# Strided sparse attention and a multiplicative FFN on one core: reordering the head's loads, casts and work

## The chip, the cores and the metric

The kernel runs on one core of one Trainium2 chip. The metric is the time of one execution on the device, in microseconds (us), as the median of several runs. The core has five engines that work side by side, each through its own queue in order: TensorE (PE, matrix multiplications and transposes into PSUM), VectorE (DVE), ScalarE (ACT), GpSimd (POOL) and SyncE (SP, which here only issues loads). 16 DMA engines move data between HBM and SBUF.

## The reference

Inputs are q, k, v of shape (8 batches, 8 heads, 576 positions, 64), and the weights w1, w2 (512 x 1024), w3 (1024 x 1024) and w_out (1024 x 512), all in float32. Heads 0 to 3 attend to the last 32 positions, heads 4 to 7 to every 32nd one back.

```
scores = q @ k.T / sqrt(64)
mask   = (0 <= i - j < 32)                   for heads 0..3
         (i >= j) and i % 32 == j % 32       for heads 4..7
attn   = softmax(where(mask, scores, -1e9)) @ v
x      = attn, heads side by side: (4608, 512)
out    = ((x @ w1) * (x @ w2)) @ w3 @ w_out  # (4608, 512)
```

## The kernel before

**The three kinds of work.** First, the *fold*: since h @ w3 @ w_out = h @ (w3 @ w_out), the kernel computes w34 = w3 @ w_out once. w3 comes in eight blocks of 128 rows (`load_w3(jc)`, called w3_0 to w3_7 in the text), w_out in four pieces (`load_wo(g)`). For a block, `fold_tr` (L357) transposes its eight 128 x 128 parts into one PSUM tile, which VectorE (L359) and ScalarE (L360) copy into w3T; `fold_mm` then multiplies w3T with w_out in two halves of four matmuls (L335, a "half step"), and the result is copied into w34 by VectorE or ScalarE. The list `fold` holds 23 units: for each block a half step, the transposes of the next block, and the other half step.

Second, *attention*, in 32 pairs of heads: pairs 0 and 1 of each batch are local, 2 and 3 strided. For a pair, `ph_T` (T) transposes q and k (L214) into one PSUM tile and copies them to qT and kT; `ph_R` (R, L230) does it for the last 64 positions of all heads of a batch; `ph_S` (S) makes the scores in two groups (L248), the exponential on ScalarE (L253) and the mask multiply on VectorE (L255); `ph_PV` (PV, L268) multiplies with v, whose extra column of ones gives the sum of the softmax, and VectorE divides (L274, L276); `ph_T2` (T2, L284) transposes the result, and a copy (L291 for strided pairs) puts it into xT. T, R and T2 share the PSUM pool psM, which has one buffer, so each waits until the one before has been copied out. S and PV share psB, which has two.

Third, the *FFN* in nine tiles of 512 tokens. `ab_halves` gives 16 units: x @ w1 (aps, L312, copied by ScalarE, L315) and x @ w2 (bps, L321, multiplied with the copy by VectorE, L323) for each of eight blocks of 128 columns. `o_halves` gives 8 units that multiply the product with w34 (L335) and store the result (L346, L347). Nine FFN tiles of 512 tokens cover eight batches of 576; the first tile needs batch 0's attention complete.

**The order of the work.** TensorE's instructions keep the order in which the program writes them. The attention phases of all batches stand in one list, `stream`; batch 0's are its first 21 units. `host(units, upto, lead)` writes out fold or FFN units one by one, and after each unit past the first `lead` ones puts in an even share of the stream units up to position `upto`. Before, batch 0's 21 units lie between fold units 4 to 23 (lead=3). In the first FFN tile, 8 units of batch 1 lie behind the ab units 10 to 16, and the remaining ones up to the end of batch 1's position (17 units) between the eight o units.

**Loads and casts.** All loads are issued by SP in the order of the calls, into the pool stgp of 9 buffers ("st"); a load waits until the cast of the load nine before has freed its buffer. A cast from float32 to float16 follows each: on GpSimd for w3, w_out, w2, q, k and the rest ("r", the last 64 positions of q and k), in `load_vL` and `load_vS` for v of the local and the strided heads; on ScalarE for w1. `copy(eng, ...)` picks the engine: "a" is L70, "v" L72 and "p" L74. The local heads' v needs a copy of its last 32 rows shifted to the first 32 partitions; that copy is on VectorE (L182). Since each engine works in order, a cast on GpSimd also waits for all casts of earlier loads.

Of the kernel before, what the change touches and what calls it, by code (L numbers as in the profile page):

```python
# [19 lines left out]
def kernel(  # L20
# [11 lines left out]
    nc = tc.nc  # L32
    B, H, S, D = q.shape
# [3 lines left out]
    P = 128  # L37
# [10 lines left out]
    LQ, LT = 96, 6  # L48
# [14 lines left out]
    AHEAD = 2  # L63

    def pe(ins):
        return tc.keep_in_program_order(ins)

    def copy(eng, out, in_):
        if eng == "a":
            nc.scalar.copy(out=out, in_=in_)  # L70
        elif eng == "v":
            nc.vector.tensor_copy(out=out, in_=in_)  # L72
        else:
            nc.gpsimd.tensor_copy(out=out, in_=in_)  # L74
# [47 lines left out]
    w1h = consts.tile([P, KM, DF], FP16)  # L122
    w2h = consts.tile([P, KM, DF], FP16)
# [9 lines left out]
    def load_wo(g, eng):  # L133
        src = moe_w_out.rearrange("(c p) n -> p c n", p=P)
        st = stgp.tile([P, 2, DM], FP32, tag="stg")
        nc.sync.dma_start(st, src[:, 2 * g:2 * g + 2, :])
        copy(eng, woh[:, 2 * g:2 * g + 2, :], st)

    def load_w3(jc, eng):
        st = stgp.tile([P, DF], FP32, tag="stg")  # L140
        nc.sync.dma_start(st, moe_w3[bass.ds(jc * P, P), :])
        t = ffn.tile([P, DF], FP16, tag="w3n", bufs=4)
        w3n[jc] = t
        copy(eng, t, st)

    def load_w12(g):
        cs = bass.ds(g * 256, 256)
        for wd, wh, eng in ((moe_w1, w1h, "a"), (moe_w2, w2h, "p")):
            st = stgp.tile([P, KM, 256], FP32, tag="stg")
            nc.sync.dma_start(st, wd.rearrange("(c p) n -> p c n", p=P)[:, :, cs])  # L150
            copy(eng, wh[:, :, cs], st)
# [4 lines left out]
    def load_qk(b, grp, engs="pp"):  # L156
        for nm, ten, eng in (("q", q, engs[0]), ("k", k, engs[1])):
            st = stgp.tile([P, 4, 4, D], FP32, tag="stg")
            nc.sync.dma_start(st.rearrange("p h c d -> p h (c d)"),
                              ten[b, 4 * grp:4 * grp + 4, 0:NM].rearrange("h (p c) d -> p h (c d)", c=4))  # L160
            t = qkp.tile([P, 4, 4, D], FP16, tag=f"{nm}{grp}")
            copy(eng, t, st.rearrange("p h c d -> p c h d"))
            x16[(b, nm, grp)] = t

    def load_rest(b, eng="p"):
        st = stgp.tile([P, H, D], FP32, tag="stg")
        for i, ten in enumerate((q, k)):
            nc.sync.dma_start(st[64 * i:64 * i + 64], ten[b, :, NM:S].rearrange("h p d -> p h d"))
        t = qkp.tile([P, H, D], FP16, tag="r")
        copy(eng, t, st)  # L170
        x16[(b, "r")] = t

    def load_vL(b):
        vt = v16L[b % 2]
        for hp in range(2):
            hs = slice(2 * hp, 2 * hp + 2)
            st = stgp.tile([P, 2, LT, D], FP32, tag="stg")
            for h in range(2):
                nc.sync.dma_start(st[32:P, h], v[b, 2 * hp + h].rearrange("(t p) d -> p t d", p=LQ))
            for pr in (bass.ds(32, 32), bass.ds(64, 64)):  # L180
                nc.gpsimd.tensor_copy(out=vt[pr, hs, :, 0:D], in_=st[pr])  # L181
            nc.vector.tensor_copy(out=vt[0:32, hs, 1:LT, 0:D], in_=vt[96:P, hs, 0:LT - 1, 0:D])  # L182

    def load_vS(b):
        vt = v16S[b % 2]
        for hp in range(2):
            st = stgp.tile([SQ, 2, ST, D], FP32, tag="stg")
            sf = st.rearrange("p h c d -> p h (c d)")
            sv = v[b, 4 + 2 * hp:6 + 2 * hp].rearrange("h (p c) d -> p h (c d)", c=ST)
            nc.sync.dma_start(sf[0:64], sv[0:64])  # L190
            nc.sync.dma_start(sf[64:SQ], sv[64:SQ])
            nc.gpsimd.tensor_copy(out=vt[:, 2 * hp:2 * hp + 2, :, 0:D], in_=st)  # L192
# [104 lines left out]
    def ab_halves(tch):  # L297
        tok = bass.ds(tch * NT, NT)
        res = []

        def first():
            abts[tch] = ffn.tile([P, KF, NT], FP16, tag="abt", bufs=4, name=f"abt{tch}")

        for jc in range(KF):
            st = {}

            def a(jc=jc, st=st):
                if jc == 0:
                    first()
                aps = psF.tile([P, NT], FP32, tag="f")  # L310
                for ci in range(KM):
                    pe(nc.tensor.matmul(aps, w1h[:, ci, bass.ds(jc * P, P)], xT[ci][:, tok],  # L312
                                        start=(ci == 0), stop=(ci == KM - 1)))
                asb = ffn.tile([P, NT], FP32, tag="asb")
                nc.scalar.copy(out=asb, in_=aps)  # L315
                st["asb"] = asb

            def bb(jc=jc, st=st):
                bps = psF.tile([P, NT], FP32, tag="f")
                for ci in range(KM):  # L320
                    pe(nc.tensor.matmul(bps, w2h[:, ci, bass.ds(jc * P, P)], xT[ci][:, tok],  # L321
                                        start=(ci == 0), stop=(ci == KM - 1)))
                nc.vector.tensor_mul(abts[tch][:, jc, :], bps, st["asb"])  # L323

            res += [a, bb]
        return res
# [45 lines left out]
    batch_end = {}  # L372
# [4 lines left out]
    for b in range(B):  # L377
# [4 lines left out]
        for i in range(4):  # L382
            p = 4 * b + i
# [14 lines left out]
    pos = [0]  # L398

    def host(units, upto, lead=0):  # L400
        n = len(units) - lead
        p0 = pos[0]
        for i, u in enumerate(units):
            u()
            tgt = p0 + ((upto - p0) * max(i + 1 - lead, 0)) // n
            while pos[0] < tgt:
                stream[pos[0]]()
                pos[0] += 1
# [2 lines left out]
    load_w3(0, "p")  # L411
    for g in range(4):
        load_wo(g, "p")
    load_w3(1, "p")
    load_qk(0, 0)
    load_rest(0)
    load_w3(2, "p")
    load_vL(0)
    load_w3(3, "p")
    load_qk(0, 1)  # L420
    load_w3(4, "p")
    load_w3(5, "p")
    load_vS(0)
    load_w3(6, "p")
    load_w3(7, "p")
    load_w12(0)
    load_w12(1)
    load_w12(2)
    load_qk(1, 0)
    load_rest(1)  # L430
    load_w12(3)
    load_vL(1)
    load_qk(1, 1)
    load_vS(1)

    fold = []
    fold_tr(0)
    for jc in range(KF):
# [2 lines left out]
        if jc + 1 < KF:  # L441
            fold.append(lambda jc=jc: fold_tr(jc + 1))
        fold.append(h1)
    host(fold, batch_end[0], lead=3)
    load_qk(2, 0)
    load_rest(2)
    load_vL(2)
    host(ab_halves(0), pos[0] + 8, lead=9)
    load_qk(2, 1)
    load_vS(2)  # L450
    host(o_halves(0), batch_end[1])
# [47 lines left out]
```

## Time and profile before

| | |
|---|---|
| median of 3 runs | 295.91 us (295.77 to 296.92) |
| span of the profiled execution | 299.8 us |
| time of the profiled execution outside its span | not recorded |
| TensorE busy | 268.9 us (90%) |
| VectorE, ScalarE, GpSimd busy | 174.6, 147.1, 102.1 us |
| first FFN tile: end of the wait for its input | 50.09 us from the span's start |
| second FFN tile: the same | 85.57 us |

The profile is of one execution, which was 3.9 us longer than the median run. It gives the busy time of each engine as a whole and in 40 slices, in which a digit is the busy share in tenths; groups of instructions by line; a timeline; and the chain of work that ended last, followed back from the last instruction through whatever released each step. A row of the chain has its start, its length in us, the engine and the line. A row of the timeline has the start, the length, the engine, the line, the operation, output and inputs, and in brackets how long the engine was idle before it and what ended that. Where the text speaks of DMA share, it is the mean busy share of the 16 DMA engines, and "granted clock" is the share of its full clock that TensorE had.

### The profile page before, as it was taken

How to read it: one execution, taken by the hardware profiler on the slowest of the kernel's cores; microseconds unless marked ns; L12 is line 12 of the kernel's file. 1: busy time of each engine (PE TensorE's matmuls, PEld its weight loads, DVE VectorE, ACT ScalarE, POOL GpSimd, SP SyncE). 2: the span in 40 equal slices, each digit the busy share in tenths (PEclk: the TensorE clock that was granted, in tenths of full speed). 3: DMA queues.
4: the chain of work that ended last, by engine and by line, in shares of the span. 5: the costliest groups of instructions: out<-in, count | busy, mean ns of one | idle time of the engine just before them, and what ended most of it. 6: DMA issues, size and time to landing. Idle time of an engine off the chain costs nothing.

```text
span 299.8 us, 6132 instructions
## 1 busy us (share of the span) xinstructions
PE 268.9 (90%) x2401; PEld 141.6 (47%) x2401; DVE 174.6 (58%) x353; ACT 147.1 (49%) x269; POOL 102.1 (34%) x118
## 2 busy tenths in 40 slices
PE   2258898989889989989999899999999999999995
PEld 1025554435545545545555445555555555444442
DVE  2011775357888866886789659747765774340430
ACT  2025586557565545536645554564455445333332
POOL 5539744486626724653455345110000000000000
PEclk9996999999999999999999999999999999999999
DMA  7999999999869929994896796030012002003003
GB/s 228 349 160 352 288 348 258 216 273 209 249 200 243 242 79 270 246 178 159 240 236 140 253 193 164 27 115 2 2 57 87 0 2 105 35 2 116 24 2 140
DMA packets 58653, 48.64 MB, mean 162 GB/s; under 512 B 29184, under 2 KB 49664, under 8 KB 58624
## 3 DMA queue, kind: packets, MB, share of 16 engines
q1 hardware_dynamic: 53440, 38.81, 54.7%
q10 hardware_dynamic: 5184, 9.44, 8.7%
q8 instruction: 19, 0.31, 0.5%
q14 instruction: 10, 0.08, 0.1%
HBM read 38.80 MB, written 9.44 MB: 161 GB/s over the span
## 4 chain that ended last, share of the span: by engine, by line
PE 67%; DVE 9%; DMA 9%; ACT 9%; issue 3%; SPq 1%; POOL 0%; ACTq 0%
PE ops L335 19%; PE bps L321 18%; PE aps L312 16%; PE xps L268 4%; PE ps L214 4%; DMA st<-in_moe_w_dram 4%; ACT pte L253 3%; DVE ptm L255 3%; DMA st<-in_moe_w_out_dram 3%; DMA out_dram<-osb 3%; PE sps L248 2%; PE ps L284 2%; DVE abt L323 2%; ACT xT L291 2%; DVE kT L72 2%
## 5 line engine op out<-in xcount | busy, mean ns | idle before, releaser
L312 PE MATMUL aps<-xT,w1h 128*128 128x512 f16 x288 | 75.3, 379 | 3.2 <-ACT xT L291 3.0
L323 DVE TENSOR_TENSOR abt<-bps,asb 128x512 f16<-128x512 f32 x72 | 49.5, 687 | 47.2 <-PE bps L321 45.5
L321 PE MATMUL bps<-xT,w2h 128*128 128x512 f16 x288 | 74.0, 379 | 0.0
L315 ACT COPY asb<-aps 128x512 f32<-128x512 f32 x72 | 42.2, 586 | 64.6 <-PE aps L312 61.8
L335 PE MATMUL ops<-w,abt 128*128 128x512 f16 x288 | 71.7, 379 | 0.5 <-DVE abt L323 0.5
L74 POOL CAST t<-st 128x1024 f16<-128x1024 f32 (+1 forms) x48 | 47.4, 991 | 43.4 <-DMA st<-in_k_dram 29.1
L253 ACT ACTIVATE pte<-sps 128x576 f16<-128x576 f32 (+1 forms) x64 | 38.4, 650 | 7.3 <-PE sps L248 7.1
L276 DVE TENSOR_TENSOR xqs<-xps,rcp 96x384 f16<-96x384 f32 (+1 forms) x64 | 39.6, 619 | 2.0
L321 PEld LDWEIGHTS <-w2h 128*128 128x128 f16 x288 | 25.8, 97 | 31.6 <-issue 5.1
L70 ACT COPY qT<-ps 128x512 f16<-128x512 f16 (+1 forms) x48 | 22.9, 481 | 29.9 <-PE ps L214 23.8
L346 ACT COPY osb<-ops 128x512 f32<-128x512 f32 x36 | 21.1, 586 | 29.9 <-PE ops L335 28.6
L335 PEld LDWEIGHTS <-abt 128*128 128x128 f16 x288 | 24.7, 98 | 23.1 <-DVE abt L323 1.0
L312 PEld LDWEIGHTS <-w1h 128*128 128x128 f16 x288 | 25.1, 98 | 22.2
L181 POOL CAST v16L<-st 32x768 f16<-32x768 f32 (+1 forms) x32 | 27.1, 847 | 18.4 <-DMA st<-in_v_dram 12.6
L268 PEld LDWEIGHTS <-ptm 72*128 72x128 f16 (+1 forms) x448 | 21.4, 97 | 19.2 <-DVE ptm L255 6.4
L255 DVE TENSOR_TENSOR ptm<-pte,maskL 128x576 f16<-128x576 f16 x32 | 20.5, 646 | 11.7 <-ACT pte L253 11.2
L72 DVE COPY kT<-ps 128x512 f16<-128x512 f16 (+1 forms) x36 | 18.8, 535 | 10.1 <-ACT qT L70 10.0
L255 DVE TENSOR_TENSOR ptm<-pte,maskS 72x576 f16<-72x576 f16 x32 | 19.6, 620 | 8.5 <-ACT pte L253 7.9
L192 POOL CAST v16S<-st 72x1024 f16<-72x1024 f32 x16 | 16.9, 1055 | 20.1 <-PE xps L268 11.4
L335 PE MATMUL ops<-woh,w3T 128*128 128x512 f16 x64 | 19.8, 440 | 3.2 <-POOL woh L74 3.1
L214 PEld LDWEIGHTS <-t 128*128 128x128 f16 x256 | 17.1, 99 | 8.8 <-issue 2.6
L214 PE MATMUL ps<-id,t 128*128 128x128 f16 x256 | 20.1, 222 | 0.5 <-POOL t L74 0.5
(48 smaller groups left out, 175.8 us busy)
## 6 DMA issues: line engine op xcount, KB each, us to landing
out_dram<-osb ACTq DMA_DIRECT2D x36, 256.0 KB, 2.0
st<-in_moe_w_dram SPq DMA_DIRECT2D x16, 512.0 KB, 8.9
st<-in_q_dram SPq DMA_DIRECT2D x16, 512.0 KB, 5.5
st<-in_k_dram SPq DMA_DIRECT2D x16, 512.0 KB, 6.6
st<-in_v_dram SPq DMA_DIRECT2D x32, 144.0 KB, 6.1
st<-in_v_dram SPq DMA_DIRECT2D x16, 256.0 KB, 7.2
st<-in_moe_w_out_dram SPq DMA_DIRECT2D x4, 512.0 KB, 8.5
st<-in_q_dram SPq DMA_DIRECT2D x8, 128.0 KB, 8.1
```

The lines of the kernel that those rows point to most:

```text
L74: nc.gpsimd.tensor_copy(out=out, in_=in_)
L181: nc.gpsimd.tensor_copy(out=vt[pr, hs, :, 0:D], in_=st[pr])
L214: pe(nc.tensor.transpose(ps[:, i, c * P:(c + 1) * P], src[:, c, h0:h0 + 2].rearrange("p h d -> p (h d)"), id16))
L253: nc.scalar.activation(out=pte[0:kr], in_=sps[0:kr, :, 0:288], func=AF.Exp, bias=0.0, scale=scale)
L255: nc.vector.tensor_mul(ptm[0:kr, 0:576].rearrange("p (a x) -> p a x", x=w), pte[0:kr].rearrange("p h (a x) -> p (h a) x", x=w), _ap(mk, 0, ...
L268: pe(nc.tensor.matmul(xps[:, h, i * 65:(i + 1) * 65], ptm[0:kr, c0:c0 + P], vt[0:kr, 2 * (s.hp % 2) + h, g * m + i, :], start=True, stop=T ...
L276: nc.vector.tensor_mul(xqs[0:w, 0:m].rearrange("p i h d -> p h i d"), xv[:, :, :, 0:D], _ap(rcp, 0, [[rp, w], [4, 2], [1, m], [0, D]]))
L312: pe(nc.tensor.matmul(aps, w1h[:, ci, bass.ds(jc * P, P)], xT[ci][:, tok], start=(ci == 0), stop=(ci == KM - 1)))
L315: nc.scalar.copy(out=asb, in_=aps)
L321: pe(nc.tensor.matmul(bps, w2h[:, ci, bass.ds(jc * P, P)], xT[ci][:, tok], start=(ci == 0), stop=(ci == KM - 1)))
L323: nc.vector.tensor_mul(abts[tch][:, jc, :], bps, st["asb"])
L335: pe(nc.tensor.matmul(st["ps"], lhs(ci), rhs(ci), start=(ci == 0), stop=(ci == KF - 1)))
```

## The change

There are three parts.

The calls of the head's loads are put in another order. Before: w3_0, w_out, w3_1, q and k of the local heads, the rest, w3_2, local v, w3_3, q and k of the strided heads, w3_4, w3_5, strided v, w3_6, w3_7, then w1 and w2. After: w3_0, w_out, w3_1 to w3_4, q and k of the local heads, the rest, local v, w3_5, w3_6, q and k of the strided heads, strided v, w3_7, then w1 and w2.

Casts go to GpSimd in the order of the loads: w1's four from ScalarE, and the shifted copies of v of batches 0 and 1, two each, from VectorE.

Batch 0's attention is placed behind fold unit 15 instead of 3, so that its 21 units lie between the last eight units of the fold; in the first FFN tile 5 instead of 8 units of batch 1 lie in the ab half, behind units 13 to 16, and 20 instead of 17 in the o half. On TensorE this puts the transposes of w3_5 and the two half steps behind them ahead of batch 0's first transposes.

```diff
     def load_w12(g):
...
-        for wd, wh, eng in ((moe_w1, w1h, "a"), (moe_w2, w2h, "p")):
+        for wd, wh, eng in ((moe_w1, w1h, "p"), (moe_w2, w2h, "p")):
...
     def load_vL(b):
...
-            nc.vector.tensor_copy(out=vt[0:32, hs, 1:LT, 0:D], in_=vt[96:P, hs, 0:LT - 1, 0:D])
+            copy("p" if b < AHEAD else "v", vt[0:32, hs, 1:LT, 0:D], vt[96:P, hs, 0:LT - 1, 0:D])
...
     load_w3(0, "p")
     for g in range(4):
         load_wo(g, "p")
-    load_w3(1, "p")
+    for jc in range(1, 5):
+        load_w3(jc, "p")
     load_qk(0, 0)
     load_rest(0)
-    load_w3(2, "p")
     load_vL(0)
-    load_w3(3, "p")
+    load_w3(5, "p")
+    load_w3(6, "p")
     load_qk(0, 1)
-    load_w3(4, "p")
-    load_w3(5, "p")
     load_vS(0)
-    load_w3(6, "p")
     load_w3(7, "p")
     load_w12(0)
...
-    host(fold, batch_end[0], lead=3)
+    host(fold, batch_end[0], lead=15)
     load_qk(2, 0)
     load_rest(2)
     load_vL(2)
-    host(ab_halves(0), pos[0] + 8, lead=9)
+    host(ab_halves(0), pos[0] + 5, lead=12)
```

## The prediction

> **What bounds the kernel now.** I read the page first (span, busy shares in 40 slices of 7.5 us), then the chain of waits in order of time for the first 90 us, then the timeline of GpSimd and of TensorE there. The page's first lines:
>
> ```profile
> span 299.8 us, 6132 instructions
> ...
> PE   2258898989889989989999899999999999999995
> ...
> PEclk9996999999999999999999999999999999999999
> ```
>
> TensorE is at 80% or more from slice 4 (22.5 us) on and at 90% over the span: what comes after the head is bound by it. The four leading digits (2, 2, 5, 8) are the head, where this change works. The chain names what the head waits for and where it ends:
>
> ```profile
> 11.61 10.69 DMA st<-in_moe_w_dram
> ...
> 23.45 1.03 PE trp L357 x8
> ...
> 28.71 0.25 PE sps L248 x6
> ...
> 49.41 0.65 ACT xT L291
> ...
> 50.09 0.38 PE aps L312
> ...
> 85.57 0.38 PE aps L312
> ```
>
> Until 23.4 the chain is a load, then its cast (22.36, 1.05), of the third block of w3 (w3_2; blocks count from 0). From 28.71 (first scores of batch 0, S0) to 50.06 it is batch 0's attention with fold matmuls between, ended by the last copy into xT; at 50.09 the first FFN tile can finish its first matmul group. At 85.57 the second tile does. So the change is worth what it does to these two marks: 50.09, and the 35.48 us from there to 85.57.
>
> The timeline of the head gives the prices:
>
> ```profile
> 15.41 3.11 PE L335 MATMUL ops<-woh,w3T 128*128 128x512 f16 x8
> ...
> 20.16 0.61 POOL L74 CAST t<-st 128x512 f16<-128x512 f32 x1 [1.03 <-DMA st<-in_k_dram]
> ...
> 23.45 1.03 PE L357 MATMUL trp<-id,t 128*128 128x128 f16 x8 [3.86 <-POOL t L74]
> 23.52 3.61 POOL L181 CAST v16L<-st 32x768 f16<-32x768 f32 x4
> ...
> 25.24 0.33 DVE L182 COPY v16L<-v16L 32x640 f16<-32x640 f16 x1 [0.29 <-POOL v16L L181]
> ```
>
> In brackets stands the idle time before, and what ended it. The casts wait for DMA: between 2 and 50 us DMA share stays about 1 whichever load is running, so the order of the loads decides what is late, not how much arrives.
>
> **The load order.** On SP's queue, and on GpSimd's with their casts, w3_2 to w3_4 pass q and k of group 0 and the rest's two DMAs; w3_3 and w3_4 also the four DMAs of the local heads' v (v below); w3_4 to w3_6 the second q and k; w3_6 also the strided heads' four v DMAs. w3_5 stays behind v. All bytes up to w3_7 are the same, so w1 and w2 (whose w2 casts wait for DMA at 41.29, 44.29, 47.27 and 57.45) land as before; the last pair was needed at 61.66, and is not the bound on either side. The staging pool has 9 buffers: q is now the tenth load and reuses w3_0's, free at 5.25; q waited for DMA until 15.39 anyway, so this costs nothing.
>
> Weights come 1.37 us apart (casts at 9.36, 10.80, 12.15, 13.48), so w3_2 to w3_4 are cast from 14.9, 16.2 and 17.6. The third block gains 7.5 us. Everything of batch 0 shifts by the three blocks, 4.1 us: the rest, cast at 20.16, is now cast at 24.3 to 24.9.
>
> **GpSimd's queue.** It works strictly in load order. Behind the rest come v's four casts (3.61), the two shifted copies that leave VectorE, then w3_5. The trace has no such copy on GpSimd. Bounds: 0.33 (VectorE alone) and 1.04 (a cast of 1024); I take 0.70, from 0.84 for 768 elements of the same partitions. The queue after the rest: 24.9 + 3.61 + 2 x 0.70 = 29.9, and up to 30.6 if v lands late; w3_5's cast ends at 30.9 to 31.7, I take 31.3. (Before, this queue ended v at 27.13.) The four w1 casts, 1.04 each, leave ScalarE (1.05 each, at 42.92, 45.62, 48.32, 57.90), where they stood among attention's copies. They add 4.2 us to GpSimd in a stretch where it is idle about half the time: nothing, unless VectorE is held up. It may be: mask multiplies (L255) take 0.46 to 1.06 in this trace, the long ones beside casts. Three more casts fall into batch 0's attention: 0 to 3 x 0.4 = 1.2 us; I take 0 as GpSimd was as busy there before.
> [...]
>
> **TensorE's fold.** It has at once what it waited for: transposes of w3_1 at 14.58, 8 matmuls to 18.5 as before, then blocks 2, 3 and 4. One block is 8 transposes and two half steps: warm 0.46 + 2 x 0.86 = 2.2, cold (as at 23.45 and 24.91) 1.03 + 3.4 = 4.4. The three end at 25.1 (warm) to 31.7 (cold). Then the program has the transposes of w3_5 **ahead of batch 0's first q/k transposes** (T0; before, T0 came behind the third half step, at 18.35). So T0, whose data are cast by 23, waits for w3_5, which stands behind v in GpSimd's queue. This is the main step: TensorE idles from 25 to 31.3. Then w3_5's transposes and two half steps: 2.2 warm to 4.2 cold (1.03 + 3.11). I take 4.2, since the 3.86 us gap before 23.45 was followed by slow rows until 28 (granted clock 0.50 from 22 to 28). T0 starts at 35.5 (33.5 to 35.9).
> [...]
>
> **Batch 0's attention.** T0 (0.5), its two ScalarE copies (1.17; the PSUM pool psM has one buffer, so the next transposes wait), R (0.4), four copies (1.0), T1 (0.6): S0 at 35.5 + 3.7 = 39.2, where before it was 28.71. From S0 to the end of xT before: 21.35 us, with 11 half steps (9.5) and 5 block transposes (2.3) between, 11.8 of filler. The fold steps that are now left behind S0 are 5 half steps and one transpose, 4.8. If all removed filler was on the path the stretch becomes 21.35 - 7.0 = 14.3; if none was, 21.4. Walking it by the new order on each engine: S0 to S1 5.2 (T1's two copies stand ahead of the exponentials on ScalarE; exp 0.66, mask 0.66, PV 0.36, half step, transposes), S1 to S2 3.5, S2 to S3 5.0 (two score buffers, each freed by a VectorE multiply of 0.69 behind a w copy), S3 to xT 4.8: 18.5, nearer the upper end because the chain through ScalarE and VectorE has little else to do and cannot be filled. xT done at 57.7, against 50.06: **+7.6**.
>
> **Tile 0.** The stream units of batch 1 in its ab half go from 8 to 5, those in its o half from 17 to 20; TensorE's work in both together is the same. Its stalls are not. Before, the ab half took 19.1 us (50.09 to 69.18) for 16 half steps of 0.86 and 3.2 of attention, so 2.1 of stalls, most where batch 1's data came late (58 to 66). Those go, since the tile starts later; but R and T1 still wait for psM (0 to 0.8), and the first PV now follows its scores with nothing between and waits for exp and mask: 1.2. So -0.9 to -0.1. The o half, with 4.16 and 3.96 of 5 us busy in 75 to 85, gets three more units beside the same matmuls: 0 to +1.5. Sum -0.9 to +1.4; I take **0**, inside both. The four shifted copies and four casts that VectorE and ScalarE lose are covered by TensorE here.
>
> **Sum.** +7.6 + 0 on the span of 299.8: 307.4. That profiled execution is 3.9 us longer than the median of the runs, 295.91; the same +7.6 there gives 303.5. Nothing after 85.57 gives it back: TensorE is busy 28 to 29.9 us of every 30, and waits there for engines, not for loads.
>
> **Rivals.**
> *Short chain.* Fold warm throughout (T0 33.5, S0 37.2) and most of the removed filler on the path (chain 16): xT at 53.2, +3.1, so 299.0. For it: ScalarE is free of its w1 casts. Against it: the gap of 6 us, and batch 1 before, whose S0 to xT, 62.62 to 85.53, took 22.9 with 9.5 of filler.
> *Long chain.* None of the filler was on the path (21.4) and masks wait for the added casts (1.2): xT at 61.8, +11.7, 307.6.
> *Faster.* One mechanism: batch 0's attention is held up mostly by the fold beside it, so that 7.0 us less fold makes its chain 14.3; with v landing 4 us sooner as well, w3_5 is cast at 27.3 and T0 starts, warm, at 29.5: S0 33.2, xT 47.5, -2.6, so 293.3. It decides when T0 to xT takes less than 50.06 less T0's start: 14.6 at my T0, where I have 22.2. Against: ScalarE was busy 1.4 to 2 of every 2 us from 42 to 50, and v ends a stretch of small packets (148 to 211 GB/s from 14 to 24 us).
> *No effect.* The head loses 2 and tile 0, whose data are then long there, gives its 2.1 of stalls back: 296. For it: the gaps in 58 to 66; they are too small for more.
>
> **How the numbers follow.** My forecast (0.58) is 303.5, itself 301 to 306. Short chain 0.18, long chain 0.12, faster 0.07, no effect 0.05. The range leaves out half the long chains and most of the faster and unchanged cases: 298.5 to 307.5. Faster by over 0.5% 0.08, within 0.5% (about what a measurement can tell, 1.5 us) 0.06, slower 0.86.
>
> **What would show it.** Right: w3_2's transposes before 19 us; a TensorE gap of some 5 us before 31, released by a cast (t, L74), cold rows behind it; T0 near 35; in 40 to 58 TensorE well under 80% busy, waiting for ptm and xT; first aps group at 57 to 58, the second tile near 93. Wrong: w3_5 cast before 28, no such gap, S0 to xT under 16, or the second tile's mark not moving with the first's.

## The result, and the profile after

The changed kernel takes 311.49 us (median of 4 runs, 307.87 to 312.94) against 296.06 for the kernel before (4 runs, 295.77 to 296.92). The ratio is 1.0507 with a 95% interval of 1.0402 to 1.0611: 15.4 us slower. The forecast, 303.5 in a range of 298.5 to 307.5, had the direction and about half the size. Ratios leave out executions that were disturbed as a whole, so here and below a ratio need not be the quotient of the medians beside it.

The profiled execution of the changed kernel spans 308.9 us; its time is 310.78, so 1.9 us lie outside a span. These are lines of its page:

```profile
span 308.9 us, 6135 instructions
...
PE   2393766898767989999999999999999999999995
...
PEclk9998699899999999999999999999999999999999
```

In slices of 7.7 us, TensorE is down in two places: slices 4 to 8 (23 to 62 us) and 10 to 13 (69 to 100 us). In the third slice (15 to 23 us) it is busier than before, 9 for 5, which is the early fold. The granted clock falls to 0.6 in slice 5. The chain of waits of the changed kernel (start, us, engine and line) shows what stands at both marks:

```profile
4.31 10.77 DMA st<-in_moe_w_dram
...
16.54 7.49 DMA st<-in_v_dram
...
28.50 0.70 POOL v16L L74
...
29.26 1.05 POOL t L74
...
30.35 1.03 PE trp L357 x8
31.39 3.41 PE ops L335 x8
34.80 0.87 PE ps L214 x8
...
58.76 0.65 ACT xT L291
...
59.44 0.38 PE aps L312
...
97.72 0.38 PE aps L312
```

The order is the forecast one: v lands, GpSimd casts and shifts it, then casts w3_5 (29.26), then w3_5's transposes and matmuls run, slow (at a granted clock of 0.50 from 30 to 35 us), and batch 0's first transposes (T0) follow. The first tile's mark is at 59.44 instead of 50.09 and the second at 97.72 instead of 85.57. But 59.44 - 50.09 is 9.35 and the times differ by 15.4. The experiments look for the rest.

### The profile page after: what moved, and what is told of

The parts are those of the page before. It is cut to its first block, busy times and chain, and to the rows that moved or that the text cites. A ratio compares the mean times of both kernels' runs of the same rounds, so it can differ in the third digit from the quotient of the medians.

```text
span 308.9 us, 6135 instructions
## 1 busy us (share of the span) xinstructions
PE 271.2 (88%) x2401; PEld 143.1 (46%) x2401; DVE 167.1 (54%) x349; ACT 143.6 (46%) x265; POOL 107.3 (35%) x126
## 4 chain that ended last, share of the span: by engine, by line
PE 69%; ACT 9%; DMA 8%; DVE 7%; issue 3%; POOL 2%; SPq 1%; POOLq 0%; ACTq 0%; DVEq 0%
PE bps L321 19%; PE aps L312 18%; PE ops L335 18%; PE xps L268 4%; PE ps L214 4%; DMA st<-in_moe_w_dram 3%; ACT pte L253 3%; DMA st<-in_v_dram 3%; PE sps L248 3%; DVE ptm L255 2%; DVE xqs L276 2%; PE ps L284 2%; ACT xT L291 2%; ACT qT L70 1%; DMA out_dram<-osb 1%
## 5 line engine op out<-in xcount | busy, mean ns | idle before, releaser
L74 POOL CAST t<-st 128x1024 f16<-128x1024 f32 (+1 forms) x48 | 46.5, 979 | 40.5 <-DMA st<-in_k_dram 28.2
L70 ACT COPY qT<-ps 128x512 f16<-128x512 f16 (+1 forms) x48 | 22.8, 481 | 28.7 <-PE ps L214 25.5
L346 ACT COPY osb<-ops 128x512 f32<-128x512 f32 x36 | 21.1, 586 | 28.2 <-PE ops L335 28.2
L268 PEld LDWEIGHTS <-ptm 72*128 72x128 f16 (+1 forms) x448 | 21.4, 99 | 25.1 <-DVE ptm L255 13.2
L192 POOL CAST v16S<-st 72x1024 f16<-72x1024 f32 x16 | 16.6, 1039 | 24.1 <-PE xps L268 18.5
L255 DVE TENSOR_TENSOR ptm<-pte,maskL 128x576 f16<-128x576 f16 x32 | 18.8, 595 | 11.2 <-ACT pte L253 10.7
L255 DVE TENSOR_TENSOR ptm<-pte,maskS 72x576 f16<-72x576 f16 x32 | 18.5, 582 | 10.8 <-ACT pte L253 10.4
L335 PE MATMUL ops<-woh,w3T 128*128 128x512 f16 x64 | 21.2, 476 | 2.0 <-POOL woh L74 1.5
L274 DVE RECIPROCAL rcp<-xps 96x6 f32<-96x6 f32 (+1 forms) x64 | 12.2, 191 | 15.5 <-PE xps L268 15.5
```

The lines of the kernel that those rows point to most:

```text
L255: nc.vector.tensor_mul(ptm[0:kr, 0:576].rearrange("p (a x) -> p a x", x=w), pte[0:kr].rearrange("p h (a x) -> p (h a) x", x=w), _ap(mk, 0, ...
L268: pe(nc.tensor.matmul(xps[:, h, i * 65:(i + 1) * 65], ptm[0:kr, c0:c0 + P], vt[0:kr, 2 * (s.hp % 2) + h, g * m + i, :], start=True, stop=T ...
L335: pe(nc.tensor.matmul(st["ps"], lhs(ci), rhs(ci), start=(ci == 0), stop=(ci == KF - 1)))
```

## The experiments

Two marks are used throughout: the end of the last copy into xT (the first tile can complete its first group) and the start of the second tile's last first-group matmul. The marks come from one profiled execution of each kernel, the last column is the median of its timed runs; "chain" is from batch 0's first scores (S0) to the end of xT.

| kernel | T0 | S0 | xT end | chain | second mark | between | behind | median us |
|---|---|---|---|---|---|---|---|---|
| before, trace of the forecast | 18.35 | 28.64 | 50.05 | 21.4 | 85.57 | 35.5 | 214.2 | 296.06 |
| before, second trace | 17.26 | 23.38 | 45.36 | 22.0 | 80.50 | 35.1 | 211.2 | 295.2 |
| new casts alone | 16.51 | 21.94 | 45.52 | 23.6 | 80.16 | 34.6 | 210.9 | 294.70 |
| new loads alone | 20.13 | 29.04 | 50.40 | 21.4 | 85.53 | 35.1 | 211.0 | 297.76 |
| new loads and casts | 18.13 | 26.66 | 48.83 | 22.2 | 84.34 | 35.5 | 210.9 | 296.93 |
| late attention alone | 33.44 | 36.99 | 58.11 | 21.1 | 93.43 | 35.3 | 210.2 | 306.29 |
| tile 0's units moved alone | 16.71 | 22.42 | 44.61 | 22.2 | 85.23 | 40.6 | 211.9 | 299.18 |
| changed, first trace | 34.59 | 38.60 | 59.40 | 20.8 | 97.72 | 38.3 | 211.2 | 311.49 |
| changed, second trace | 33.40 | 36.96 | 58.45 | 21.5 | 100.29 | 41.8 | 210.9 | 309.92 |
| changed, tile 0 as before | 33.53 | 37.09 | 57.12 | 20.0 | 91.87 | 34.8 | 210.7 | 304.16 |
| changed, w3_5 ahead of v | 27.39 | 33.25 | 56.00 | 22.8 | 96.17 | 40.2 | 209.9 | 305.16 |
| changed, gap filled | 31.62 | 35.17 | 57.68 | 22.5 | 97.59 | 39.9 | 210.0 | 310.66 |
| changed, no fold in attention | 33.76 | 37.67 | 56.24 | 18.6 | 101.26 | 45.0 | 209.9 | 313.06 |
| tile 0's units moved the other way | 16.62 | 22.57 | 47.69 | 25.1 | 82.75 | 35.1 | 211.5 | 298.70 |

"Between" is the second mark less the end of xT, "behind" the span less the second mark. Where no fold is in attention, "between" has the fold written behind it in it.

**A second trace of before.** The same kernel, nothing edited.

> The kernel before, unchanged, for a second trace. The profiled execution of before spanned 299.8 us, the changed kernel's 308.9 at a time of 310.78, so 1.9 us lie outside a span; by that the timed runs of before (296.06) span about 294, 5.7 us less than the trace on which the forecast rests. Theory 1 (that trace was an ordinary head and an unusually slow later part): marks of the first and second tile at 50 and 85.5 again, the rest some 208 us. Theory 2 (its head was slow): first mark near 45, the second near 80, the rest 214.

It took 295.2 us (ratio 1.0024, 0.9969 to 1.0079). Lines of its page, and of its chain of waits:

```profile
span 291.7 us, 6132 instructions
...
PEclk9999999999999999999999999999999999999999
```

```profile
45.41 0.38 PE aps L312
...
80.50 0.38 PE aps L312
```

Mostly theory 2: of the 8.1 us between the two spans, 4.7 lie ahead of the first mark, 0.4 between the marks and 3.0 behind. In the trace of the forecast w3_2's transposes began at 23.45 after 3.86 us of idleness; here they do at 19.72 after 1.40, as this timeline of TensorE shows:

```profile
17.26 1.06 PE L214 MATMUL ps<-id,t 128*128 128x128 f16 x8
19.72 0.62 PE L357 MATMUL trp<-id,t 128*128 128x128 f16 x8 [1.40 <-POOL t L74]
...
23.38 0.43 PE L248 MATMUL sps<-qT,kT 64*128 64x96 f16 x12
```

From 14 to 24 us the DMA engines moved 263 GB/s here and 180 there, at nearly the same DMA share (1.19 and 1.15), and the granted clock was 1.00 here and 0.50 from 22 to 28 there. So one kernel has heads that differ by 5 us. Why the 3.0 us behind the second mark differ was not looked into. The median run of before lies between the two executions (293.39 and some 301.7 us). Against this trace the change costs 17.2 us of span (308.9 - 291.7): 14.0 ahead of the first mark, 3.2 between the marks, 0.0 behind them.

**New loads and new casts, old places.**

```diff
-    host(fold, batch_end[0], lead=15)
+    host(fold, batch_end[0], lead=3)
...
-    host(ab_halves(0), pos[0] + 5, lead=12)
+    host(ab_halves(0), pos[0] + 8, lead=9)
```

(against the changed kernel)

> The new load order and the casts on GpSimd, with attention where it stood before (first units behind fold unit 3, eight units of batch 1 in the first tile). Theory (the late placing of batch 0's attention costs the head its 9 us): batch 0's q and k come 3 to 4 us later, but the fold keeps filling TensorE; first tile's mark at 50 to 53, time 295 to 299. Rival (late data of batch 0 or casts on GpSimd are the cost): mark at 56 to 59, time 304 to 310.

296.93 us, ratio 1.0092 (1.0038 to 1.0145); xT ends at 48.83. The loads and casts cost little. Each alone, against before:

> Before with the new load order alone. Theory (batch 0's data come 4 us later, and part of that lies on the path since attention's chain is the longest thing in the head): first mark 2 to 4 us later than in the second trace of before (45.4), time 1 to 3.5 us above before. Rival (fold matmuls fill the time): mark within 1 us.

> Before with only the casts of w1 and the shifted copies of v of batches 0 and 1 on GpSimd. Theory (covered on both sides): marks within 1 us, time 294.5 to 296.5. Rival (the added GpSimd work delays q, k and v and blocks VectorE's mask multiplies): first mark 2 to 4 us later, time 297 to 299.

The load order alone: 297.76, ratio 1.0024 (0.9988 to 1.0060). Its trace has xT at 50.40 with a slow stretch of its own (two half steps from 24.7 to 29 us took 1.91 and 1.83 instead of 1.03), as the first trace of before has one, so the mark of one trace settles nothing here; the medians leave 1.6 us. The casts alone: 294.70, ratio 1.0123 (0.9945 to 1.0300), an unclear result around no change; the marks agree with the second trace of before within 0.4 us. The new copy on GpSimd takes 0.72 us.

**Late attention alone.**

```diff
-    host(fold, batch_end[0], lead=3)
+    host(fold, batch_end[0], lead=15)
```

(against before, with the old loads and casts)

> The old load order and casts; only batch 0's attention is placed behind fold unit 15. Theory: w3_5 is cast at 34, cold transposes and half steps follow, first q and k transposes near 37, then a chain of 21 us as in the changed kernel: mark at 60 to 62, time 306 to 309. Rival (load order is the cost): mark within 3 us of before, time 295 to 299.

306.29 us, ratio 1.0420 (1.0328 to 1.0513). That is 10.8 us above the median of before in the same set of runs (295.51), the largest part of the loss. T0 is at 33.44 though its q and k were cast by 16.57, no later than in the trace of the forecast (19.13). In the timeline of TensorE the w3 blocks are waited for one by one, each behind its cast, and T0 stands behind all of them:

```profile
25.28 0.62 PE L357 MATMUL trp<-id,t 128*128 128x128 f16 x8 [1.38 <-POOL t L74]
...
31.26 0.62 PE L357 MATMUL trp<-id,t 128*128 128x128 f16 x8 [0.22 <-POOL t L74]
31.71 1.89 PE L335 MATMUL ops<-woh,w3T 128*128 128x512 f16 x8
33.44 0.61 PE L214 MATMUL ps<-id,t 128*128 128x128 f16 x8
```

**Tile 0's units moved, alone and undone.** Against before, and against the changed kernel in the other direction:

```diff
-    host(ab_halves(0), pos[0] + 8, lead=9)
+    host(ab_halves(0), pos[0] + 5, lead=12)
```

> Before, with only the first tile's attention moved: 5 instead of 8 units of batch 1 in its ab half, 20 instead of 17 in its o half. Theory (denser attention beside the o half stalls TensorE): the stretch from the first tile's mark to the second's grows by 2 to 4 us, time 298 to 300. Rival (the late data of batch 1 set this stretch before, so less attention in the ab half gains what the o half loses): no change, 295.5 to 297.

> The changed kernel with the first tile's attention as before (8 units of batch 1 in the ab half, 17 in the o half). Theory (the dense o half costs what it cost alone, 3.7 us of time): stretch between the two marks 35 to 36, time 306.5 to 309. Rival (with a late head, batch 1's data are in time and the placement no longer matters): stretch 37 to 38.5, time 310 to 312.

Alone it costs 3.7 us by the medians (299.18 against 295.51), ratio 1.0186 (1.0073 to 1.0298), and the stretch between the marks goes from 35.1 to 40.6. Undone in the changed kernel, the stretch is 34.8 and the time 304.16 (ratio to before 1.0424, 1.0286 to 1.0561). Part of the 40.6 is the clock: in that trace the granted clock was 0.60 and 0.54 from 68 to 72 us (the half step at 69.68 took 1.91), while it was 1.00 in this stretch of the first trace of the changed kernel and of the run with the units moved back. The stalls are in the o half. Of the longest waits in the changed kernel from 76.2 to 97.7, and after that in the second trace of before from 63.7 to 80.5 (engine, line, what it waited for: us, times, longest), these are the ones of PV's matmuls (PE) and their weight loads (PEld) for the masked exponentials:

```profile
PEld L268 <- DVE ptm L255: 6.3, 6, 1.3
...
PE xps L268 <- DVE ptm L255: 4.7, 6, 1.1
```

```profile
PEld L268 <- DVE ptm L255: 2.3, 5, 0.8
...
PE xps L268 <- DVE ptm L255: 0.6, 1, 0.6
```

TensorE was busy 15.33 of those 21.5 us, and 14.20 of 16.8 before, so it was idle 6.2 us instead of 2.6. By these waits, with 20 units between eight half steps, a pair's scores and the PV that needs them have too little between them to cover exp and mask.

**The same, the other way.** Before with the new casts, and

```diff
-    host(ab_halves(0), pos[0] + 8, lead=9)
+    host(ab_halves(0), pos[0] + 11, lead=6)
```

> Before with the casts on GpSimd and the first tile's attention moved the other way: 11 units of batch 1 in the ab half (behind units 7 to 16), 14 in the o half. Theory (each three units moved out of the o half spare what moving three in cost): stretch between the marks 32.5 to 34.5 instead of 35, time 1 to 2.5 us under before. Rival (batch 1's k and v land too late for it): stretch 35 to 38, time 0 to 3 us above before.

298.70, ratio 1.0079 (1.0037 to 1.0121), between the marks 35.1: the rival. Its chain of waits runs through batch 1's v:

```profile
47.18 7.28 DMA st<-in_v_dram
```

so in this stretch the loads are the limit in that direction, and the dense o half in the other. What this run loses lies ahead of the first mark: xT ends at 47.69, and at 45.52 with the casts alone. The granted clock was 0.67 and 0.50 from 26 to 30 us here and 1.00 there (half steps of 1.81 and 1.79 us, and of 1.03).

**w3_5 ahead of v.** Against the changed kernel:

```diff
     load_rest(0)
-    load_vL(0)
     load_w3(5, "p")
+    load_vL(0)
     load_w3(6, "p")
```

> The changed kernel with w3_5's load moved ahead of the local heads' v, so that its cast no longer stands behind v's casts. Theory (T0 waits for w3_5 in GpSimd's queue): TensorE's gap before 30 shrinks from 5 to under 1.5 us, no cold rows, T0 at 27 to 28.5 instead of 34.6, first tile's mark at 51 to 54, time 303 to 306. Rival (batch 0's data or the chain's other inputs hold it): mark moves by less than 2 us, time 309 to 311.

305.16 us, ratio to before 1.0449 (1.0309 to 1.0589). TensorE's timeline:

```profile
25.21 0.62 PE L357 MATMUL trp<-id,t 128*128 128x128 f16 x8 [0.51 <-POOL t L74]
25.66 1.89 PE L335 MATMUL ops<-woh,w3T 128*128 128x512 f16 x8
27.39 0.61 PE L214 MATMUL ps<-id,t 128*128 128x128 f16 x8
29.16 0.38 PE L230 MATMUL ps<-id,t 128*128 128x128 f16 x4 [1.16 <-ACT kT L70]
31.78 0.68 PE L357 MATMUL trp<-id,t 128*128 128x128 f16 x8 [2.23 <-POOL t L74]
```

The gap of 5 us is 0.51, nothing behind it is slow up to T0 (0.62 and 1.89 instead of 1.03 and 3.62; the granted clock was 1.00 from 27 to 32), and T0 starts at 27.39, 7.2 us earlier, so the cause named for the gap is shown. Part of the gain goes at once: the next transposes, of w3_6, wait 2.23 us for their own cast behind v, ahead of T1, and S0 is only 5.4 us earlier. By xT 3.4 are left, since the chain took 22.8 us instead of 20.8, at a mean granted clock of 0.72 instead of 0.92. The end of xT, 56.00, fell short of the theory's 51 to 54: w3_5 was the first of a row of waits and not the only one.

**The gap filled.** Against the changed kernel, 24 extra matmuls ahead of w3_5's transposes:

```diff
+    def warm():
+        ps = psF.tile([P, NT], FP32, tag="f", name="warm")
+        for _ in range(24):
+            pe(nc.tensor.matmul(ps, id16, woh[:, 0, :], start=True, stop=True))
+
+    tr5 = fold[13]
+    fold[13] = lambda: (warm(), tr5())
     host(fold, batch_end[0], lead=15)
```

> The changed kernel with 24 matmuls of 0.216 us, whose result nothing reads, written into TensorE's gap before w3_5's transposes. They are extra work and leave the output alone. Theory (the gap lets the clock fall, and the steps behind it run at half speed): w3_5's transposes take 0.6 and its eight matmuls 1.9 instead of 1.0 and 3.6, T0 is 2 us earlier, first mark 2 to 3 us earlier, time 2 to 4 us under the changed kernel's in the same call. Rival (the half-speed stretch is hidden beside the waits for casts and for ScalarE): less than 1 us.

Its four times, 306.03 to 312.69 (median 310.66), cannot be told from the changed kernel's beside them, 309.77 to 313.11 (309.92); a gain of 2 us is not ruled out. Its timeline of TensorE:

```profile
29.43 0.62 PE L357 MATMUL trp<-id,t 128*128 128x128 f16 x8 [0.63 <-POOL t L74]
29.89 1.89 PE L335 MATMUL ops<-woh,w3T 128*128 128x512 f16 x8
31.62 0.61 PE L214 MATMUL ps<-id,t 128*128 128x128 f16 x8
...
38.17 1.90 PE L335 MATMUL ops<-woh,w3T 128*128 128x512 f16 x4
```

The steps behind the gap run at full speed (a granted clock of 1.00 from 28 to 36 us) and T0 is 1.8 us earlier than in the second trace of the changed kernel, as the theory had it, but xT only 0.8. The slow clock comes later instead, inside attention (0.50 from 38 to 42): the half step at 38.17 takes 1.90 us, where the one in the first trace, at full clock, took 1.02. Six traces have attention late and the same fold in the chain. In them the chain took 20.0 to 21.1 us at a mean granted clock of 0.91 to 0.92, 21.5 at 0.80 (the second trace of the changed kernel), and 22.5 and 22.8 at 0.77 and 0.72 (this run and the one before). So the half-speed stretch at 30 is real, but taking it away moves the end of xT by 0.8 us against the second trace and 1.7 against the first, of the 9 to 14 that the change costs there.

**No fold inside attention.** Against the changed kernel:

```diff
-    host(fold, batch_end[0], lead=15)
+    for u in fold[:16]:
+        u()
+    while pos[0] < batch_end[0]:
+        stream[pos[0]]()
+        pos[0] += 1
+    for u in fold[16:]:
+        u()
```

> The changed kernel with the seven fold units that lie in batch 0's attention written behind it instead, so that attention has nothing beside it on TensorE. First q/k transposes (T0) as in the changed kernel, near 34.6. Theory (attention's chain through ScalarE and VectorE sets its length, and fold beside it is hidden): first scores to the last copy into xT still takes 18 to 20 us (20.8 with the seven units, 22.0 in the second trace of before with sixteen), and the 5.2 us of fold are now on the path: first tile's mark at 62 to 65, time 314 to 317. Rival (the fold units lengthen the chain): 14 to 16 us, mark 59 to 60, time 310 to 312.

313.06 us, ratio 1.0709 (1.0637 to 1.0782). The chain takes 18.6 us with no fold unit in it, 20.8 and 21.5 with five half steps and one transpose, 21.4 and 22.0 with eleven and five. TensorE's timeline where it begins and ends:

```profile
37.67 0.49 PE L248 MATMUL sps<-qT,kT 64*128 64x96 f16 x12
...
39.95 0.51 PE L268 MATMUL xps<-v16L,ptm 128*128 128x65 f16 x6 [1.79 <-ACT pte L253]
41.16 0.51 PE L268 MATMUL xps<-v16L,ptm 128*128 128x65 f16 x6 [0.70 <-DVE ptm L255]
...
55.14 0.42 PE L284 MATMUL ps<-id,xqs 72*128 72x72 f16 x4 [0.41 <-DVE xqs L276]
55.37 1.05 PE L357 MATMUL trp<-id,t 128*128 128x128 f16 x8
```

So in these traces 11.8 us of fold cost the chain some 3 us. What TensorE waits for in it are ScalarE's exponentials and copies (kT: 0.57 and 0.40 us) and VectorE's masks and divisions, one after another, and beside them it has room for some 9 us of other work (an estimate, 11.8 less 3). This chain ran at half clock from 38 to 56 us, so at full clock it may be shorter, and the fold's cost larger; how much was not tried. The other runs of the table spread as well: 20.0 to 22.8 us with attention late, 21.4 to 25.1 with attention early.

**A second trace of the changed kernel.**

> The changed kernel, unchanged, for a second trace and as the neighbour of the next run. Theory (its loss sits in the head and the first tile): marks at 57 to 60 and 95 to 98, 210 to 212 us behind them, time 307 to 313. Rival (the first trace's head was unusual, as that of before was): first mark under 56.

309.92 us, ratio 1.0498 (1.0442 to 1.0554), xT at 58.45 and the second mark at 100.29: the first trace was ordinary, except that the stretch between the marks is 3.5 us longer here. Its granted clock was between 0.50 and 0.83 from 76 to 82 us (half steps of 1.78 and 1.42 us), and 1.00 in the whole stretch of the first trace. By the medians the parts add up: 10.8 (late attention) + 3.7 (tile 0) + 1.4 (loads and casts) = 15.9, against 15.4 and 13.8 in the two comparisons. By the ratios they are 4.2 + 1.9 + 0.9 = 7.0%, against 5.1% and 5.0%, so the sizes of the parts are known to a few us only; that late attention is the largest holds either way. No version here beats before by more than can be measured.

## Why the prediction was wrong

**The load order: right in direction.** w3_2 to w3_4 were cast from 13.85, 15.13 and 16.52 (forecast 14.9, 16.2, 17.6), the rest at 22.26 (24.3). All came 1 to 2 us sooner than forecast, as in the second trace of before. w1 and w2 were indeed no bound: the last of their casts ended at 55.42, ahead of the first mark. The prediction's step from a DMA share of about 1 to a fixed amount that arrives does not hold: the two traces of before moved 180 and 263 GB/s at a share of 1.15 and 1.19.

**GpSimd's queue and T0: right.** The shifted copy took 0.72 (0.70), w3_5's cast ended at 30.31 (31.3), TensorE's gap ended on it, and the two steps behind it ran slow: T0 at 34.59 (35.5), S0 at 38.60 (39.2). The run with w3_5 ahead of v shows the cause. In the first trace an idle gap of 5.19 us was followed by slow rows until T0, at a granted clock of 0.50 from 30 to 35 us.

**Batch 0's attention: mis-sized.** I took 18.5 us for the chain, between 14.3 (all removed fold on the path) and 21.4 (none). It took 20.8: nearly none was. The step that failed is "18.5, nearer the upper end": the walk along the rows of single operations came out 2.3 us short, probably because it left out waits between them (which ones was not traced), and the whole row I had, 21.35 with 11.8 of fold beside it, was nearly the answer. The rival called *Long chain* was the right one on this point. Its other half, masks that wait for the added casts, is not shown: the chain's eight mask multiplies took 6.5 and 4.5 us in the two traces of the changed kernel and 5.1 and 6.6 in the two of before, so they vary as much without the added casts. (The trace of the forecast has masks of up to 1.30 us, not 1.06.)

**Tile 0: wrong.** I set 0 between -0.9 and +1.4. Against the second trace of before it was +3.2 and +6.7 in the two traces, and 5.5 for that edit alone. The step that failed is the o half's "0 to +1.5". In the first trace of the changed kernel TensorE is idle 6.2 us in the o half, and 2.1 in that of the trace of the forecast (14.28 busy of 16.39): +4.1. The three units were priced as work beside the same matmuls, while the wait for the masked exponentials grew as the spacing shrank (PV's matmuls: 4.7 us against 0.6 in the second trace of before). The ab half went about as forecast, idle 1.5 us instead of 2.2. And a late start alone spares this stretch next to nothing: with tile 0 as before, the late head's stretch is 34.8 against 35.1.

**The sum: the largest error.** "The same +7.6 there gives 303.5" carried a difference from one execution to the median. The 3.9 us between them compares a span, 299.8, with a time, 295.91; with some 1.9 outside its span that execution was 5.6 us slower than the median of 296.06, and 4.7 of what set it apart from the second trace lay in the very stretch that the change replaces, a slow head with a half-clock stretch of its own (0.50 from 22 to 28 us). The changed kernel's first mark came at nearly the same place in both of its traces (59.40 and 58.45), while that of before moved from 50.05 to 45.36. So the comparison with the slow head most likely hid that much of the cost; with two traces of each kernel this is argued and not shown. Against the trace of the forecast, the terms were +7.6 forecast and +9.3 measured for the head, 0 and +2.8 for tile 0 (35.48 to 38.28), 0 and -3.0 for what follows: 9.1 of span. The times differ by 15.4: to the 9.1 come the 5.6 by which the one execution was slow and 0.7 by which the changed kernel's median lies above its own profiled execution. The number 3.9 that I set beside it should have been a warning: the slowest of the three runs was 296.92.

## What to carry to other kernels

A long dependent chain that goes through several engines is shortened little by taking other work out of it (here 3 us for 11.8 of work); it is mostly started earlier or later, so such a chain belongs as early as its data allow, with the independent work put into its gaps. Ahead of moving steps on an in-order engine, look at which input each step ahead of the chain's first one waits for, and through which in-order queue that input comes (with late attention alone T0 ran at 33.44, its q and k cast by 16.57). And a difference to one profiled execution counts for the median only if that execution's time is near it; where its time is off, find the stretch that makes it so before pricing a change there.

## What the runs showed of the hardware that was not expected

TensorE's clock fell without any long gap. With no fold inside attention the granted clock was 0.50 from 38 to 56 us, while no idle time of TensorE in it exceeded 1.79 us and it was busy 2.4 to 3.2 us of every 4 from 40 on:

```profile
40.00:44.00 4.00, 2.74 (x37) 2.27 (x38) 2.42 (x5) 1.44 (x3) 2.87 (x4) 0.50 1.09 348
44.00:48.00 4.00, 2.82 (x41) 2.16 (x39) 2.90 (x6) 2.08 (x5) 2.35 (x3) 0.50 1.20 259
```

(columns: stretch, length, busy time and instructions of TensorE, its weight loads, VectorE, ScalarE and GpSimd, granted clock, DMA share, GB/s). In the run with w3_5 ahead of v it fell between 32 and 33 us, after four microseconds with gaps of 1.16 and 2.23 in which it was busy 0.6. So the clock can fall with no gap as long as the 3.86 and 5.19 us that stood ahead of the slow rows at 23 and 30 us in the first traces of before and of the changed kernel. How empty a stretch must be is not shown: in the run with the casts alone TensorE was busy 1.1 of the 4 us from 22 to 26, and in the first trace of the changed kernel 1.8 of those from 36 to 40, and in neither did the clock fall in the eight us that followed (half steps of 1.02 to 1.04 us in the one, a granted clock of 1.00 in the other).
